# Two more attention pairs on the DMA-transpose path: batch 1, pairs 4 and 5

## The chip, the cores and the metric

One core of a Trainium2 chip runs the whole kernel. The time is device microseconds from launch to end, as the median of several runs. The engines named below are the matmul engine (PE, with its weight loads as PEld), the vector engine (DVE), the scalar engine (ACT), GpSimd (POOL) and the sync engine (SP, which here only issues DMA). Times inside the profile count from the first instruction of the profiled execution.

## The reference

Eight batches of 12 heads, 448 rows, head size 64. Attention with normalized queries and keys, then a low-rank mixing along the sequence, then a two-layer channel network with a residual:

```python
q_n = q / (norm(q) + 1e-6);  k_n = k / (norm(k) + 1e-6)
attn = softmax(q_n @ k_n.T / tau)            # per head, 448 x 448
x = concat_heads(attn @ v)                   # 448 x 768 per batch
u = x + (x.T @ U @ V).T                      # U: 448 x 32, V: 32 x 448
out = u + relu(u @ w_ch1) @ w_ch2            # w_ch1: 768 x 3072, w_ch2: 3072 x 768
```

## The kernel before

The work is cut into 48 **pairs** of heads, numbered `n = 6 * batch + pair` (`NP = 6`), so that batch 1 is n = 6 to 11. One pair takes these steps:

- **Preparation** on a group of two pairs (`Prep`, group 6 is n = 10 and 11, group 7 is n = 12 and 13): squares on POOL, sums on DVE (`reduce`), the root on ACT (`root`), the reciprocal on DVE (`invert`), then four scalings on POOL (`scale`, line 268) that write the normalized `qk`, and a cast of the values on POOL (`values`).
- **T**: the turn of `qk` into `qkT`. For pairs below `2 * NP` this is eight PE transposes (line 297) and a DVE copy (line 302). For pairs from `2 * NP` on, `by_dma` is true and it is one DMA transpose issued by SP (line 312).
- **Sc**: scores, four chunks of keys, each followed by an exponential on ACT. **V**: attention times values in two halves (lines 373 and 380), each divided by its row sums on DVE (`divide_V`, lines 391 and 392) into `X`.
- **Mixing**. The early way is one pair at a time (`step_A`, `step_H`): four matmuls with U (line 413), four that turn X (line 427), one with V (line 438), and a DVE copy to `u` (line 443). The late way (`step_XT`, `step_A2`, `step_H2`) turns X by DMA (line 458), and mixes two pairs as a couple with small matmuls placed side by side (lines 466 and 480), then adds the turned X on DVE (line 485).

Between these steps PE does the channel network of the batch before, cut into **fill** steps of six matmuls: M1 (line 510, w_ch1 with N = 448) and M2 (line 537, w_ch2 with N = 384). M2 of one output half needs that half of w_ch2, loaded by POOL's queue with a cast (`load_w2`, line 173) in two parts of 12 row blocks.

The order on every engine is written by hand. The main loop runs over n from 6; for each n a list `order` holds steps with weights, and `spread` hands out fill between them by these weights. The dictionary `after` holds side work put at (n, place): the preparations, the loads, and the DMA transposes. A queue executes in program order, so a waiting instruction holds those behind it. `FIRST2` decides from which n the couple way and its own `order` lists are used (`late = n > FIRST2`), and `KEEP = 3` fill steps are held back over a batch's end, to cover the last couple's `H2`.

In batch 1 the fill is the channel network of batch 0. So n = 9 is where M2 of batch 0 starts, with the first half of w_ch2; the second half is needed in n = 11.

Of the kernel before, what the change touches and what calls it, by code (L numbers as in the profile page):

```python
# [22 lines left out]
def kernel(  # L23
# [23 lines left out]
    NP = H // 2  # L47
# [123 lines left out]
    def load_w2(half, n0, n1):  # L171
        cols = slice(half * HC, (half + 1) * HC)
        nc.gpsimd.dma_start(
            out=w2_sb[:, n0:n1, cols],
            in_=moe_w_ch2[n0 * 128:n1 * 128, cols].rearrange("(n p) d -> p n d", p=128))
# [100 lines left out]
            nc.gpsimd.tensor_copy(out=self.flat(v65[self.s])[:, :, 0:D], in_=self.flat(vst[self.s]))  # L276


    qkT = {}

    def by_dma(n):

        return n >= 2 * NP

    tp_of, sc_of = {}, {}

# [19 lines left out]
    def step_T(b, p):  # L306
        if not by_dma(b * NP + p):
            pe_T(b, p)
            evict_T(b, p)
            return  # L310
        gi, j = group_of[(b, p)]
        nc.sync.dma_start_transpose(
            out=new_qkT(b, p).rearrange("p a (c r) -> p (a c) r", r=128),
            in_=norm[gi][0][:, j, :, :, :, :].rearrange("p i c h d -> p (i c h d)"))
# [17 lines left out]
    def step_S3(b, p):  # L332

        for i, (nm, tag) in enumerate((("av", "ps_av"), ("up", "ps_x"))):
            t = qkT[(b, p + i)]
            bank = psum.tile([128, 512], FP, name=nm, tag=tag, bufs=1)
            sc_of[(b, p + i, 3)] = bank.unsqueeze(1)
            for h in range(2):
                r, o = slice(64 * h, 64 * h + 64), 64 * (h ^ i)
                nc.tensor.matmul(out=bank[o:o + 64, 0:S], lhsT=t[r, 1, 384 + o:448 + o],  # L340
                                 rhs=t[r, 0, 0:S], start=True, stop=True)
        est.pe(0.19)
        for i in range(2):
            exp_S(b, p + i, 3)

    def exp_S(b, p, c):
        e = E[(b * NP + p) % 2]
        sc = sc_of.pop((b, p, c))
        if c == 3:
            nc.scalar.activation(out=last_of(b, p)[:, 0:S], in_=sc[:, 0, 0:S], func=AF.Exp)  # L350
            est.act(0.56)
        else:
            nc.scalar.activation(out=e[:, 2 * c:2 * c + 2, 0:S], in_=sc[:, :, 0:S], func=AF.Exp)  # L353
            est.act(0.93)

    def step_S(b, p, cs):
        for c in cs:
            pe_S(b, p, c)
            exp_S(b, p, c)
# [217 lines left out]
    pairs = [(b, p) for b in range(B) for p in range(NP)]  # L577
# [9 lines left out]
    def load_all(gi):  # L587
        if gi < len(groups):
            for x in ("q", "k", "v"):
                load(gi, x, nc.sync)  # L590
# [13 lines left out]
    def T(n):  # L604
        step_T(*pairs[n])

    def Sc(n, *cs):
        step_S(*pairs[n], cs)

    def V(n, half):  # L610
        step_V(*pairs[n], half)

    def A(n):
        step_A(*pairs[n])

    def Hs(n):
        step_H(*pairs[n])
# [112 lines left out]
    def put(n, at, fn):  # L730
        after.setdefault((n, at), []).append(fn)

    for gi in range(5, len(groups)):
        m, g = first_pair[gi], preps[gi]
        if m == NP + 2:
            at = [(NP, 1), (NP, 2), (NP + 1, 6), (NP, 5), (NP + 1, 0), (NP + 1, 1)]
            when = (NP + 1, 2)
        elif m == NP + 4:
            at = [(NP + 2, 0), (NP + 2, 1), (NP + 2, 6), (NP + 2, 4), (NP + 2, 6), (NP + 2, 7)]
            when = (NP + 3, 0)  # L740
        elif m == 2 * NP:
            at = [(m - 3, 6), (m - 2, 0), (m - 1, 0)] + [(m - 2, i) for i in (1, 3, 4)]
            when = (m - 2, 5)
        elif m == 2 * NP + 2:
            at = [(m - 2, i) for i in (0, 0, 6, 3, 4, 5)]
            when = (m - 2, 6)
        else:
            at = [(m - 3, 0), (m - 3, 0), (m - 3, 5)] + [(m - 2, i) for i in (0, 1, 2)]
            when = (m - 2, 3)

        put(*at[0], lambda g=g: g.square(0))
        put(*at[1], lambda g=g: g.square(1))
        put(*at[2], lambda g=g: g.values())
        put(*at[3], lambda g=g: g.reduce(0))
        put(*at[4], lambda g=g: g.reduce(1))
        put(*at[5], lambda g=g: g.root())
        put(*when, lambda g=g: (g.invert(), [g.scale(i, j, P_) for j in (0, 1) for i in (1, 0)]))
        if gi > 5 and m - 6 <= NP:
            put(*((NP, 3), (NP + 3, 0))[gi - 6], lambda gi=gi: load_all(gi))
        elif gi > 5:  # L760
            at = {2 * NP + 2: [(m - 4, 5), (m - 4, 6), (m - 3, 2)],
                  2 * NP + 4: [(m - 4, i) for i in (0, 2, 4)]}.get(m, [(m - 6, 4), (m - 5, 5), (m - 4, 3)])
            for x, w in zip("qkv", at):
                put(*w, lambda gi=gi, x=x: load(gi, x, nc.sync))
        if by_dma(m):
            put(m - 1, -1, lambda m=m: T(m))
            put(m - 1, 0, lambda m=m: T(m + 1))

    put(NP, 2, lambda: load_w1(2304, 3072))
    put(NP, 3, lambda: (load_w2(0, 0, 12), load_w2(0, 12, 24)))  # L770
    put(NP + 1, 2, lambda: (load_w2(1, 0, 12), load_w2(1, 12, 24)))
    put(NP + 3, 0, load_copies)
    put(NP + 5, 6, place_copies)

    def spread(n, order, nf, first=0):

# [9 lines left out]
            f(min(want - given, len(fill)))  # L786
            given = want

    FIRST2 = 2 * NP
    KEEP = 3  # L790
    for n in range(NP, NPAIR + 1):
        b, p = pairs[n] if n < NPAIR else (B, 0)
        now, nxt = n < NPAIR, n + 1 < NPAIR
        done = n > NP
        late = n > FIRST2
        for g in after.pop((n, -1), []):
            g()
        state_of["busy"] = n == NP + 1
        if not late:
            if n % 2 == 0:  # L800

                order = [
                    (1, lambda: Sc(n, 0, 1)),
                    (0, done and (lambda: V(n - 1, 0))),
                    (1, None if by_dma(n + 1) else (lambda: T(n + 1))),
                    (0, lambda: Sc(n, 3)),
                    (1, (lambda: V(n - 1, 1)) if done else None),
                    (0, done and (lambda: A(n - 1))),
                    (1, lambda: (Sc(n, 2), Sc(n + 1, 0))),
                    (1, (lambda: Hs(n - 1)) if done else None),  # L810
                ]
            else:
                order = [
                    (1, lambda: Sc(n, 1, 2)),
                    (1, lambda: V(n - 1, 0)),
                    (0, lambda: Sc(n, 3)),
                    (1, lambda: V(n - 1, 1)),
                    (1, not by_dma(n + 1) and (lambda: T(n + 1))),
                    (1, lambda: A(n - 1)),
                    (0, lambda: Hs(n - 1)),  # L820
                ]
            last = p == 0 and done
            nf = len(fill) if last else 5
            spread(n, order, nf)
            if last:
                f(len(fill))
                fill.extend(steps_m1(b - 1) + steps_m2(b - 1))
            continue

        def X2(m):  # L830
            step_XT(*pairs[m])

        def A2(m):
            step_A2(*pairs[m])

        def H2(m):
            step_H2(*pairs[m])

        if n % 2 == 0:
            order = [  # L840
                (2, now and (lambda: (step_S3(*pairs[n]), Sc(n, 0, 1)))),
                (2, lambda: V(n - 1, 0)),
                (2, lambda: (V(n - 1, 1), X2(n - 1))),
                (2, None),
                (3, lambda: (A2(n - 2), now and (Sc(n, 2), Sc(n + 1, 0)))),
                (2, not now and (lambda: H2(n - 2))),
            ]
            nf = len(fill) if not now else int(round((len(fill) - KEEP) / (1 + (-p) % NP)))
            spread(n, order, nf)
            if not now:  # L850
                f(len(fill))
                fill.extend(steps_m1(b - 1) + steps_m2(b - 1))
            continue
        Sc(n, 1, 2)
        if n - 3 >= FIRST2:
            H2(n - 3)
        for g in after.pop((n, 0), []):
            g()
        if p == 1 and n - 2 > FIRST2:
            f(len(fill))  # L860
            fill.extend(steps_m1(b - 1) + steps_m2(b - 1))
        order = [
            (2, lambda: V(n - 1, 0)),
            (2, None if n > FIRST2 + 1 else (lambda: Sc(n, 3))),
            (2, lambda: (V(n - 1, 1), X2(n - 1))),
            (2, None),
            (2, None),
        ]
        nf = int(round((len(fill) - KEEP) / (1 + (-p) % NP)))
        f(2)  # L870
        spread(n, order, nf - 2, 1)
# [37 lines left out]
```

## Time and profile before

| what | value |
|---|---|
| median of 3 runs | 583.81 us (583.78 to 583.82) |
| profiled span | 581.2 us |
| PE busy | 569.7 us, 98% of the span |
| DVE, ACT, POOL busy | 214.3, 260.7, 215.3 us |
| granted PE clock | 0.998 |
| DMA transposes of qk | 36, landing in 3.1 to 6.0 us |
| loads of a quarter of w_ch2 | 4, landing in 23.3 to 31.1 us |

PE is busy nearly always, and matmuls are pipelined, so its busy time says little of lost time. What is lost is read from the chain of waits and from the distance between the starts of neighbouring matmuls.

In the trace the steps of the stretch concerned start at these times on PE: n = 8 at 63.4 us, n = 9 at 72.5, n = 10 at 81.0, n = 11 at 90.8, n = 12 at 98.3, n = 13 at 112.5.

### The profile page before, as it was taken

What the parts mean: (1) busy time and instruction counts of PE and PEld (TensorE: products, weight loads), DVE (VectorE), ACT (ScalarE), POOL (GpSimd) and SP (SyncE); (2) the same over time, 40 slices, a digit from 0 to 9 for tenths busy, and PEclk for the clock granted to TensorE, in tenths of its full rate; (3) what the DMA queues carried; (4) which work ended last, traced back from release to release, by engine and by line L of the source; (5) the groups of instructions that cost most, each with busy time, mean ns of one, the idle gap of its engine ahead of it and who ended that gap; (6) DMA issues with size and microseconds to landing.
All of it is one profiled execution on the core that took longest, in us unless ns stands there. A gap on an engine that the chain in (4) does not pass through costs nothing.

```text
span 581.2 us, 12255 instructions
## 1 busy us (share of the span) xinstructions
PE 569.7 (98%) x5080; PEld 328.7 (57%) x5080; DVE 214.3 (37%) x462; ACT 260.7 (45%) x447; POOL 215.3 (37%) x205
## 2 busy tenths in 40 slices
PE   7999999999999999999999999999999999999997
PEld 6665556655565556555655555655566555655564
DVE  7874552433243334423324343432244332320011
ACT  5877545455433554446424455246443374214200
POOL 8754865706326146326055163253261420000000
PEclk9999999999999999999999999999999999999999
DMA  6899999646376485585375663773754640231012
GB/s 165 195 248 236 239 210 223 178 95 137 98 162 145 93 158 112 135 163 112 80 160 133 132 137 96 144 175 79 136 131 111 132 74 18 52 74 32 11 45 56
DMA packets 138585, 74.25 MB, mean 128 GB/s; under 512 B 85568, under 2 KB 138352, under 8 KB 138528
## 3 DMA queue, kind: packets, MB, share of 16 engines
q1 hardware_dynamic: 128256, 62.77, 48.9%
q0 software_dynamic: 9728, 10.18, 10.3%
q8 instruction: 40, 0.66, 0.5%
q10 hardware_dynamic: 544, 0.51, 0.3%
q14 instruction: 17, 0.14, 0.1%
HBM read 52.19 MB, written 11.01 MB: 109 GB/s over the span
## 4 chain that ended last, share of the span: by engine, by line
PE 89%; DMA 6%; DVE 2%; ACT 1%; SPq 1%; POOL 1%; issue 0%; DVEq 0%; ACTq 0%
PE mp L537 38%; PE mp L510 34%; PE sc L328 5%; DMA w_sb<-in_moe_w_ch_dram 5%; PE av L380 3%; PE up L380 2%; PE av L373 1%; PE av L340 1%; PE sc L650 1%; PE up L373 1%; PE up L466 1%; DMA qst<-in_q_dram 1%; DVE ss L248 1%; PE av L480 1%; PE tp L297 0%; DVE qkT L302 0%
## 5 line engine op out<-in xcount | busy, mean ns | idle before, releaser
L537 PE MATMUL mp<-w_sb,relu 128*128 128x384 bf16 x1344 | 233.7, 326 | 0.2 <-DMA w_sb<-in_moe_w_ch_dram 0.2
L537 PEld LDWEIGHTS <-relu 128*128 128x128 bf16 x1344 | 125.3, 98 | 89.3 <-issue 13.1
L510 PEld LDWEIGHTS <-w_sb 128*128 128x128 bf16 x1128 | 105.0, 98 | 99.5 <-issue 10.0
L514 ACT ACTIVATE relu<-mp 128x448 bf16<-128x448 f32 x161 | 87.6, 544 | 127.8 <-PE mp L510 127.8
L268 POOL TENSOR_TENSOR qk<-kst,inv 128x512 bf16<-128x512 f32 x43 | 46.0, 1070 | 241.9 <-DVE inv L262 241.9
L353 ACT ACTIVATE E<-sc 128x896 bf16<-128x896 f32 x144 | 125.1, 922 | 21.9 <-PE sc L328 20.8
L510 PE MATMUL mp<-uO,w_sb 128*128 128x448 bf16 x576 | 114.3, 353 | 0.0
L510 PE MATMUL mp<-uE,w_sb 128*128 128x448 bf16 x552 | 112.9, 353 | 0.0
L555 DVE TENSOR_TENSOR o_sb<-mp,ut 128x384 f32<-128x384 f32 x50 | 27.9, 558 | 141.3 <-PE mp L537 137.1
L248 DVE TENSOR_REDUCE ss<-sq 128x16 f32<-128x1024 f32 (+1 forms) x50 | 57.9, 1165 | 0.8 <-ACT sq L240 0.7
L268 POOL TENSOR_TENSOR qk<-qst,inv 128x512 bf16<-128x512 f32 x44 | 47.4, 1078 | 1.6 <-PE up L438 1.6
L516 DVE TENSOR_SCALAR relu<-mp 128x448 bf16<-128x448 f32 x27 | 16.9, 625 | 81.2 <-PE mp L510 80.7
L380 PEld LDWEIGHTS <-E 128*128 128x128 bf16 x1152 | 45.0, 97 | 0.0
L328 PE MATMUL sc<-qkT 64*64 64x448 bf16 x576 | 42.4, 359 | 0.6 <-ACT E L353 0.3
L243 POOL TENSOR_TENSOR sq<-kst 128x1024 f32<-128x1024 f32 (+1 forms) x23 | 42.7, 1858 | 0.1
L243 POOL TENSOR_TENSOR sq<-qst 128x1024 f32<-128x1024 f32 x21 | 39.9, 1900 | 3.2 <-DMA qst<-in_q_dram 3.2
L350 ACT ACTIVATE E<-av 128x448 bf16<-128x448 f32 x17 | 9.2, 541 | 47.3 <-PE up L340 47.3
L380 PE MATMUL av<-v,E 128*128 128x65 bf16 x648 | 29.1, 193 | 0.0
L276 POOL CAST v<-vst 128x1024 bf16<-128x1024 f32 (+1 forms) x25 | 25.1, 1006 | 7.7 <-DMA vst<-in_v_dram 6.1
L373 PEld LDWEIGHTS <-E 128*128 128x128 bf16 x192 | 18.1, 98 | 14.7 <-issue 0.8
L470 ACT CAST A_sb<-up 128x128 bf16<-128x128 f32 x18 | 4.8, 264 | 45.9 <-PE up L466 45.9
L391 DVE RECIPROCAL rd<-av 128x4 f32<-128x4 f32 x54 | 9.7, 180 | 42.3 <-PE av L380 42.3
(99 smaller groups left out, 351.2 us busy)
## 6 DMA issues: line engine op xcount, KB each, us to landing
out_dram<-o_sb SPq DMA_DIRECT2D x109, 96.0 KB, 2.2
w_sb<-in_moe_w_ch_dram POOLq DMA_DIRECT2D x8, 1152.0 KB, 18.5
qst<-in_q_dram SPq DMA_DIRECT2D x23, 256.0 KB, 3.8
vst<-in_v_dram SPq DMA_DIRECT2D x46, 128.0 KB, 2.9
kst<-in_k_dram SPq DMA_DIRECT2D x44, 128.0 KB, 2.8
qst<-in_q_dram SPq DMA_DIRECT2D x23, 192.0 KB, 4.0
vst<-in_v_dram SPq DMA_DIRECT2D x46, 96.0 KB, 2.7
kst<-in_k_dram SPq DMA_DIRECT2D x44, 96.0 KB, 2.7
```

The lines of the kernel that those rows point to most:

```text
L243: nc.gpsimd.tensor_mul(sq[:, 0:self.nh * 4, :], self.flat(t), self.flat(t))
L248: nc.vector.reduce_sum(self.ss[:, j, 0:self.nh * 4], self.sq[j][:, 0:self.nh * 4, :], axis=AX.X)
L268: eng.tensor_mul(qks[self.gi % 2][:, j, i, :, :, :], t[:, 2 * j:2 * j + 2, :, :].rearrange("p h c d -> p c h d"), iv.unsqueeze(3).to_broad ...
L276: nc.gpsimd.tensor_copy(out=self.flat(v65[self.s])[:, :, 0:D], in_=self.flat(vst[self.s]))
L328: nc.tensor.matmul(out=sc[o:o + 64, h, 0:S], lhsT=t[r, 1, c * 128 + o:c * 128 + o + 64], rhs=t[r, 0, 0:S], start=True, stop=True)
L353: nc.scalar.activation(out=e[:, 2 * c:2 * c + 2, 0:S], in_=sc[:, :, 0:S], func=AF.Exp)
L373: nc.tensor.matmul(out=av[:, i, :, :], lhsT=last_of(b, p)[:, ic * 128:(ic + 1) * 128], rhs=vv[:, 2 * j:2 * j + 2, 3, :], start=(i == 0), s ...
L380: nc.tensor.matmul(out=av[:, i, h, :], lhsT=e[:, 2 * c + h, ic * 128:(ic + 1) * 128], rhs=vv[:, 2 * j + h, c, :], start=False, stop=(i == ...
L510: nc.tensor.matmul(out=mp, lhsT=w1_sb[:, cc, f * 128:(f + 1) * 128], rhs=u[:, cc, 0:S], start=(cc == 0), stop=(cc == CC - 1))
L514: nc.scalar.activation(out=relu[:, f, o:o + S], in_=mp, func=AF.Relu)
L537: nc.tensor.matmul(out=mp, lhsT=relu[:, f, r0:r0 + 128], rhs=w2_sb[:, f, half * HC:(half + 1) * HC], start=(f == 0), stop=(b > 0 and f == ...
L555: nc.vector.tensor_add(o.rearrange("p (k d) -> p k d", d=128), mp.rearrange("p (k d) -> p k d", d=128), ut_of[(b, half)][:, :, c, :])
```

## The change

Pairs 10 and 11 (the last two of batch 1) go to the late way: their `qk` is turned by two DMA transposes in place of 16 PE transposes and two DVE copies, and they are mixed as a couple, their X turned by DMA. For this the code splits the old bound in two: `FIRST2 = NP + 4` for the turn and the couple, and `FIRST4 = 2 * NP + 2` for the fourth score chunk, which stays as it was for n = 10 to 13.

So that the DMA transposes of 10 and 11 can be issued in n = 9, group 6 is prepared sooner (all of it in n = 8), and group 7 too; the load of the second half of w_ch2 moves from n = 7 to n = 8, behind the squares of group 6, so that POOL has these done first.

```diff
+    FIRST2 = NP + 4
+    FIRST4 = 2 * NP + 2
     def by_dma(n):
-        return n >= 2 * NP
+        return n >= FIRST2
...
         if m == NP + 2:
-            at = [(NP, 1), (NP, 2), (NP + 1, 6), (NP, 5), (NP + 1, 0), (NP + 1, 1)]
+            at = [(NP, 1), (NP, 2), (NP + 2, 1), (NP, 5), (NP + 1, 0), (NP + 1, 1)]
             when = (NP + 1, 2)
         elif m == NP + 4:
-            at = [(NP + 2, 0), (NP + 2, 1), (NP + 2, 6), (NP + 2, 4), (NP + 2, 6), (NP + 2, 7)]
-            when = (NP + 3, 0)
+            at = [(NP + 2, 0), (NP + 2, 0), (NP + 2, 6), (NP + 2, 3), (NP + 2, 4), (NP + 2, 5)]
+            when = (NP + 2, 6)
         elif m == 2 * NP:
-            at = [(m - 3, 6), (m - 2, 0), (m - 1, 0)] + [(m - 2, i) for i in (1, 3, 4)]
+            at = [(m - 3, 6), (m - 3, 6), (m - 1, 0)] + [(m - 2, i) for i in (0, 1, 2)]
+            when = (m - 2, 3)
+        elif m == 2 * NP + 2:
+            at = [(m - 2, i) for i in (0, 0, 5, 2, 3, 4)]
             when = (m - 2, 5)
-        elif m == 2 * NP + 2:
-            at = [(m - 2, i) for i in (0, 0, 6, 3, 4, 5)]
-            when = (m - 2, 6)
...
         if by_dma(m):
-            put(m - 1, -1, lambda m=m: T(m))
-            put(m - 1, 0, lambda m=m: T(m + 1))
+            put(m - 1, 1 if m == FIRST2 else -1, lambda m=m: T(m))
+            put(m - 1, 3 if m == FIRST2 else 0, lambda m=m: T(m + 1))
...
-    put(NP + 1, 2, lambda: (load_w2(1, 0, 12), load_w2(1, 12, 24)))
+    put(NP + 2, 1, lambda: (load_w2(1, 0, 12), load_w2(1, 12, 24)))
...
-    put(NP + 5, 6, place_copies)
+    put(NP + 5, 5, place_copies)
...
-    FIRST2 = 2 * NP
...
-                (2, now and (lambda: (step_S3(*pairs[n]), Sc(n, 0, 1)))),
+                (2, now and (lambda: (n >= FIRST4 and step_S3(*pairs[n]), Sc(n, 0, 1)))),
...
-                (2, None),
+                (2, None if n >= FIRST4 else (lambda: Sc(n, 3))),
...
-            (2, None if n > FIRST2 + 1 else (lambda: Sc(n, 3))),
+            (2, None if n > FIRST4 else (lambda: Sc(n, 3))),
```

The list `at` gives the places of: squares of q, squares of k, values, sums of q, sums of k, root; `when` is the place of the reciprocal and the four scalings. With `late` true from n = 11, batch 0's last fill is now shared out as 6 steps in n = 11, 7 in n = 12 and the 3 kept ones at the start of n = 13, where it was 5 and 11.

More of the change, by code (lines that the diff above doesn't have):

```diff
@@ L817 @@
                     (1, lambda: V(n - 1, 1)),
-                    (1, not by_dma(n + 1) and (lambda: T(n + 1))),
+                    (1, None if by_dma(n + 1) else (lambda: T(n + 1))),
                     (1, lambda: A(n - 1)),
```

## The prediction

> **What bounds the kernel now.** I read the shares of the chain that ended last, then the same chain in order of time around the edited steps, then what PE waited for, then the DMA queues in the same stretch. The chain's shares by engine:
>
> ```profile
> PE 89%; DMA 6%; DVE 2%; ACT 1%; SPq 1%; POOL 1%; issue 0%; DVEq 0%; ACTq 0%
> ```
>
> PE sets the end, but not alone: DMA and DVE hold parts of the chain. The chain in order of time (start, length, what) shows where:
>
> ```profile
> 50.13 29.54 DMA w_sb<-in_moe_w_ch_dram
> 79.71 1.14 PE mp L537 x6
> 80.84 0.19 PE up L438
> 81.03 0.50 PE sc L328 x8
> 81.54 1.08 PE mp L537 x6
> 82.62 0.18 PE mp L547 x3
> 82.82 0.56 DVE o_sb L553
> 83.38 0.13 DVE rd L391
> 83.54 0.42 DVE X L392
> 83.96 1.13 DVE ss L248
> 85.09 0.60 DVE qkT L302
> 85.69 1.13 DVE ss L248
> 86.94 0.44 DVE X L392
> 87.41 0.38 PE av L413 x4
> ```
>
> Two links matter. The second part of w_ch2's first half, issued at 50.13, lands at 79.67, and the third M2 step of batch 0 starts on it at 79.71. So whatever PE saves between 50 and 79.7 us is lost again in this wait. Then DVE carries the path from 82.82 to 87.41: A of pair 9 (line 413) waits for X of pair 9, which stands behind two sums and the qkT copy of pair 11. What PE lost there:
>
> ```profile
> PE av L413 <- DVE X L392: 1.1, 1, 1.1
> PE mp L537 <- DMA w_sb<-in_moe_w_ch_dram: 0.2, 1, 0.2
> ```
>
> By the starts of neighbouring matmuls the two cost 1.22 us (1.378 where 0.162 is usual) and 0.39 us (0.422 where 0.028 is usual). After 113 us I find no start later than its usual distance, up to the end; so the result is the shift of n = 13, and nothing later adds to it.
>
> The DMA queues, first in 62 to 72 us, then in 76 to 80, then in 96 to 98 (packets, MB, share):
>
> ```profile
> q0 software_dynamic: 1532, 1.16, 74.1%
> q1 hardware_dynamic: 1506, 1.23, 48.3%
> ...
> q0 software_dynamic: 1070, 0.81, 130.6%
> q1 hardware_dynamic: 11, 0.01, 0.9%
> ...
> q1 hardware_dynamic: 1614, 0.40, 90.9%
> ```
>
> The reader is to see that the rings are never idle before 94 us, that POOL's queue (q0, the weights) and SP's (q1) go packet for packet while both have work, and that alone a weight packet takes 4 us x 16 / 1070 = 60 ns of one ring. In 96 to 98 us it is the transposes of pairs 12 and 13, which the packet records show as 1024 packets of 256 B each; about 14 ns a packet, 0.9 us a transpose, with the rings to themselves.
>
> **What the Trainium skill says.** "TensorE: Matmul & The Clock Gate", Part 1: warm matmuls start N / 2.4 + about 2.5 ns apart; the trace agrees (56 ns for N = 128, 189 for 448, 162 for 384). "TensorEngine Tiling (Array Packing)", Key Properties: changing the tiling mode drains the engine; the trace agrees (256 ns from an M2 matmul to a 64x64 one, where 162 is usual). "DMA: Bandwidth & Descriptors", Queues, rings and completion order: each DMA engine takes turns between the queues it has work for, packet by packet; the equal counts above agree. The same page, SWDGE vs HWDGE vs iDMA: a packet may hold several descriptors, up to 4096 B; no run here shows how many a transpose has.
>
> **The change part by part.**
>
> *PE work.* Removed: 16 transposes x 56 ns = 0.90 us; two A of 4 x 56 = 0.45; two turns of X of 0.19 = 0.39; two H of 0.189 = 0.38; sum 2.12. Added: one A2 (eight small matmuls, and the mode changes before and after; 0.23 more than the mode changes it replaces) and one H2 of 0.19, together 0.42. I counted the built order of PE with the trace's usual distance for each neighbouring pair: 569.04 us before, 567.34 after, with the wait of 79.7 taken out of its class. So **1.70 us** less, of which T of pair 10 (0.45) comes before the wait at 79.7, T of pair 11 (0.44) lies beside the DVE chain, and 0.81 comes after 87.4.
>
> *T of pair 10 off PE.* PE reaches the third M2 step 0.45 us sooner (78.84) and waits there for the weights. Worth nothing by itself.
>
> *DVE chain to A of pair 9.* In the built order sums of q now go before o_sb, beside other work; then o_sb, X, sums of k, the wait for root on ACT, the two operations of invert, and only then the second X. From the start of o_sb: 0.56 + 0.16 + 0.42 + 1.13, root 0.62 with its hand-overs (86.81 to 87.43 before), invert 0.55, reciprocal and X 0.63, hand-over 0.05: 4.12 us, where it was 87.41 - 82.82 = 4.59. So the wait stays (PE would be there 1.17 us earlier), and **0.47 us** is gained where 0.44 of PE work was removed. E of chunk 3 stands behind root on ACT; it is needed only by V of pair 10, 5 us later.
>
> *Couple mixing after 87.4.* **0.81 us**, straight off PE, if nothing waits. X by DMA: issued near 99 and 105, landing some 2.5 to 4 us later (2.5 is the median), needed at about 110. H2's adds on DVE (2 x 0.62) and the copy of 1.02 lie beside the three kept M2 steps (2.9 us), as in all later batches. The bank `up` for the second half of V is free then.
>
> *Earlier group 6.* Squares at 62.1 to 65.9 on POOL, sums at 67.0 and 68.7 on DVE, root near 69.9, invert until 71.1, scalings 71.15 to 75.2. The first sum goes before X of pair 7, which ends at about 68.71 where it ended at 68.66; A of pair 7 is at 68.96: no wait. The exponentials of n = 8 go 0.6 us later on ACT; their banks are needed at 72.5 and free at 72.15. Nothing.
>
> *Second half of w_ch2 issued at 67 instead of 62.* It stands in POOL's queue behind the first half, which ends at 79.67 either way: it landed at 85.41 and 94.27, is needed at about 96 and 99. Nothing.
>
> *DMA transposes of 10 and 11.* This is the new cost. Issued at 73.3 and 75.3, behind value loads in q1 whose last ring lands at 76.93, and in turn with the end of the very weights that PE waits for. On the slowest ring some 2.6 us of weights are left at 76.5. Low end, one for one at 60 + 16 = 76 ns: 43 packets x 16 = 0.7 us later. High end, transposes in bundles: both get through first, 1.8 us later. The transpose of 10 itself then ends at 76.5 + 64 x 76 ns = 81.4, lands about 0.6 later at 82.0, while Sc of pair 10 wants it at 80.96. No transpose runs beside weights in this trace, so this is bounded, not read. I take 1.1 us for the larger of the two delays (0 to 2.5 for the range). Behind Sc wait V of pair 9, o_sb and so the whole DVE chain. Pair 11 lands near 87, needed at 88 or later: hidden.
>
> *Transposes of 12 and 13.* They landed at 97.53 and 98.42, and Sc of 12 came at 98.28, a margin of 0.75. The two new transposes add 2 x 64 x 14 to 20 ns = 1.8 to 2.6 us to each ring before them: landing 99.3 to 100.1. Sc of 12 now comes at 98.28 + 1.1 - 0.47 - 0.61 + 0.97 (one more fill step ahead of it) = 99.3. Wait 0 to 0.9; I take 0.4.
>
> Sum: -0.47 - 0.81 + 1.1 + 0.4 = +0.2 us: **584.0 us**.
>
> **The rivals.**
>
> *A, the transposes ride for free*: the weights land as before, pair 10 in time, pair 12 in time. Then -0.47 - 0.81 = -1.28: **582.5 us**, 0.22% faster. For it: a transpose needs only 0.9 us of the rings. Against: the rings are full.
>
> *B, a new wait takes the place*: the transposes lose more against the weights, at 100 ns and more a packet, or hold up the rings (in 94 to 96 us pair 12's first half went, and the rest only when the last ring was free). Then delay 2.5 and wait 0.9 and up: +2.1 and more, **586.0 us**, slower. For it: a load that shares the rings takes 104 ns a turn. Against: loads are three to four times larger than these packets.
>
> *C, both old waits vanish*: -1.70 - 0.39 - 1.22 = -3.3, **580.5 us**. It needs the weights sooner, and nothing in their queue before them changes.
>
> **How the numbers follow.** The forecast's case (from -1.1 to +1.1 us) gets 0.46, A 0.20, B 0.30, C 0.04. Range 582.4 to 586.0: it takes in A and most of B, and leaves out C and the worst of B. Faster is A and C, 0.24; slower is B, 0.30.
>
> **What would show it.** Right: M2's wait on the weights over 0.5 us, PE's wait for X near 1.2 still there, a wait of Sc on qkT by DMA at 81 to 83 us, a landing of pair 10's transpose over 5 us, no wait after n = 13. Wrong: weights that land before 79.9 and pair 10 before 80.9 (A), or a wait of over 1.5 us on qkT at n = 10, 11 or 12 (B), or a wait of H2 for the turned X, which I took as hidden.

## The result, and the profile after

| | median us | ratio to before, 95% interval |
|---|---|---|
| before | 583.79 | |
| the change, 4 executions | 586.10 (585.77 to 587.43) | 1.0048 (1.0029 to 1.0066) |
| the change again, 22 executions | 586.17 (585.57 to 588.16) | 1.0036 (1.0023 to 1.0049) |

The change makes the kernel 0.4% slower, about 2.4 us. Both intervals leave out "no difference". The profiled span is 585.6 us (before 581.2). The profiled execution of the change is the slowest of the four (587.43 us, the others 585.77 to 586.19), so its trace shows more than the median loss.

Although 22 matmuls fewer are recorded, PE's busy time rises from 569.7 to 571.6 us. Two rows of the page of after, the span in 40 slices of 14.6 us, show where to look (PE's busy tenths, and the clock that PE was granted):

```profile
PE   7999979999999999999999999999999999999997
PEclk9999989999999999999999999999999999999999
```

The sixth slice, 73 to 88 us, has both a PE that stands still and a clock that is not full. In the page of before the same clock digit is a 9. What PE waited for, in after (total, times, longest, in us):

```profile
PE mp L539 <- DMA w_sb<-in_moe_w_ch_dram: 3.8, 1, 3.8
...
PE av L415 <- DVE X L394: 0.9, 1, 0.9
```

Before, the same two rows had 0.2 and 1.1. The chain of waits of after, in order of time, from the landing of the weights on:

```profile
51.65 31.43 DMA w_sb<-in_moe_w_ch_dram
83.08 0.04 issue
83.12 2.08 PE mp L539 x6
85.20 0.37 PE up L440
85.57 0.89 PE sc L330 x8
86.47 2.04 PE mp L539 x6
88.50 0.32 PE mp L549 x3
...
92.53 0.43 DVE X L394
92.96 0.04 issue
93.00 0.38 PE av L415 x4
```

The second part of w_ch2's first half lands at 83.08, where before it was 79.67. And every PE step after it has about twice its usual length: six M2 matmuls take 2.08 us, not the 1.14 that they took before, and the eight score matmuls 0.89, not 0.50. By the stretches of the trace of after (length, then busy time and instructions of PE, PEld, DVE, ACT, POOL; then PE's clock, the DMA share and GB/s):

```profile
76.50:79.50 3.00, 2.84 (x34) 1.97 (x32) 0.61 (x2) 1.06 (x3) 2.99 (x4) 1.00 1.28 206
82.10:88.90 6.80, 5.78 (x27) 2.55 (x27) 1.79 (x3) 1.73 (x2) 0.00 (x0) 0.50 1.29 193
88.90:93.00 4.10, 3.17 (x41) 2.14 (x39) 3.24 (x8) 0.98 (x3) 0.40 (x1) 0.99 1.30 197
```

For 6.8 us the granted clock is 0.50. Neighbouring M2 matmuls are then 320 ns apart instead of 162. So a busy PE is here a slow PE: the rise in busy time is no added work.

The queues of after in 78 to 84 us (packets, MB, share of 16 engines):

```profile
q0 software_dynamic: 1114, 0.84, 91.0%
q1 hardware_dynamic: 1112, 0.28, 38.4%
```

q0 holds the weights, q1 the two transposes. They get the rings in equal numbers of packets, 1114 to 1112. A pair of packets takes 6 us x 16 / 1113 = 86 ns of a ring, where a weight packet alone took 60. So each 256-byte transpose packet costs the weights about 26 ns, and costs its own transfer 86 ns.

Where the time came in, by the starts of PE's steps in the profiled executions (us; the distances are worked out from them). The third and fifth columns belong to experiments told below: the couple mixing and the sooner preparation with the turn left on PE, and the change with filler work in the wait.

| | before | couple, turn on PE | the change | with filler | the change again |
|---|---|---|---|---|---|
| start of n = 9 | 72.54 | 73.00 | 72.84 | 72.45 | 72.40 |
| to Sc of pair 10 | 8.42 | 8.88 | 12.66 | 12.42 | 11.15 |
| from there to A of pair 9 | 6.45 | 5.88 | 7.50 | 5.88 | 7.76 |
| from there to n = 11 | 3.43 | 3.43 | 3.43 | 3.43 | 3.43 |
| from there to n = 12 | 7.44 | 7.80 | 7.88 | 7.80 | 8.18 |

Two rows carry the loss. Sc of pair 10 comes later, because of the transfers; in the first trace of the change 1.1 us of it is the clock already, since from the M2 step that waited to Sc of pair 10 it took 2.38 us (83.12 to 85.50) where the kernel with the turn on PE took 1.26 (80.62 to 81.88). And from there to A of pair 9 the change takes longer than that kernel, because of the clock. The last row holds one more fill step from the new shares (0.97 us). After n = 13 no start is later than its usual distance, in any of these traces.

### The profile page after: what moved, and what is told of

Its sections match the earlier page's. It is cut to its first block, busy times and chain, and to the rows that moved or that the text cites. A ratio compares the mean times of both kernels' runs of the same rounds, so it can differ in the third digit from the quotient of the medians.

```text
span 585.6 us, 12219 instructions
## 1 busy us (share of the span) xinstructions
PE 571.6 (98%) x5058; PEld 328.4 (56%) x5058; DVE 212.3 (36%) x459; ACT 261.1 (45%) x447; POOL 215.2 (37%) x205
## 3 DMA queue, kind: packets, MB, share of 16 engines
q0 software_dynamic: 9728, 10.18, 10.3%
## 4 chain that ended last, share of the span: by engine, by line
PE 87%; DMA 7%; SPq 2%; DVE 1%; POOL 1%; ACT 1%; issue 1%; POOLq 0%; DVEq 0%
PE mp L539 38%; PE mp L512 33%; DMA w_sb<-in_moe_w_ch_dram 5%; PE sc L330 5%; PE av L382 3%; PE up L382 2%; DMA kst<-in_k_dram 1%; PE av L375 1%; PE av L342 1%; PE up L375 1%; PE up L468 1%; PE av L482 1%; DMA vst<-in_v_dram 1%; SPq L213 0%; DVE X L394 0%
## 5 line engine op out<-in xcount | busy, mean ns | idle before, releaser
L375 PEld LDWEIGHTS <-E 128*128 128x128 bf16 x192 | 18.1, 98 | 14.6 <-issue 1.0
```

Source lines behind the costliest of these rows:

```text
L375: nc.tensor.matmul(out=av[:, i, :, :], lhsT=last_of(b, p)[:, ic * 128:(ic + 1) * 128], rhs=vv[:, 2 * j:2 * j + 2, 3, :], start=(i == 0), s ...
```

## The experiments

My theory after the result: the loss is the DMA turn alone, first by the ring time that it takes from the weights, then by the clock that drops in the wait; the couple mixing and the sooner preparation gain what I had worked out. The rivals: the couple mixing or the new places of the preparation cost something; or the loss is in what waits for `qkT`, not in the ring time.

**One part undone: the turn back on PE.** Couple mixing and preparation stay.

```diff
     def by_dma(n):
-        return n >= FIRST2
+        return n >= 2 * NP
...
-        if half == 1 and by_dma(b * NP + p):
+        if half == 1 and b * NP + p >= FIRST2:
```

> The change, but pairs 10 and 11 are turned by PE as before; the couple mixing, the X turned by DMA and the earlier preparation stay. Contention theory (the two new DMA transposes take turns with the first half of w_ch2 on the rings and so lengthen PE's wait for it): the weights' second part lands as in the kernel before (near 79.7, within 1 us), and the time is 0.3 to 1.3 us below before, 582.5 to 583.5. Rival, couple mixing (H2 or A2 waits, KEEP too small): slower than before by 1.5 us or more, like the change. Rival, preparation order: slower as well.

Measured: 582.17 us, ratio 0.9972 (0.996 to 0.9983): faster than before by 1.5 us, a little more than expected. PE's waits in this kernel:

```profile
PE mp L539 <- DMA w_sb<-in_moe_w_ch_dram: 0.7, 1, 0.7
...
PE av L415 <- DVE X L394: 0.5, 1, 0.5
```

The wait on the weights is 0.7 us instead of 3.8, and that on X of pair 9 is half of what it was before the change. So the turn by DMA costs (1.0036 - 0.9972) x 583.7 = 3.7 us, by the measurement of the change with more executions, and the rest of the change is a gain.

**The other part undone: single mixing, turn by DMA.**

```diff
-    FIRST2 = NP + 4
+    FIRST2 = 2 * NP
...
     def by_dma(n):
-        return n >= FIRST2
+        return n >= NP + 4
...
```

The lines left out keep the places of the two transposes and of the bank for V as these bounds ask.

> The change, but pairs 10 and 11 are mixed one at a time as before; their turn by DMA and the earlier preparation stay. Contention theory: PE waits over 2 us for the weights at the third M2 step, pair 10's transpose takes over 9 us to land, and the time is 2 to 4 us above before, 585.8 to 587.8. Rival, couple mixing: no slower than before.

Measured: 587.58 us, 1.0068 (1.0055 to 1.0081). In its trace PE waited 2.8 us for the weights and 2.1 for `qkT` in two waits, and the clock was halved for 3.4 us. Without the couple mixing the change is slower still, by (1.0068 - 1.0036) x 583.7 = 1.9 us. That is more than the 0.8 of PE work that the mixing saves; part of it is a wait of 1.6 us for the turn of pair 12, which ended at 103.66 us; in the two traces of the change that wait is 0.1 and 0.4. The rest was not followed up.

**The cost alone: the kernel before, with two more transposes that nobody reads.** They turn `qk` of pairs 8 and 9 once more (the second in two halves), into tiles that are not read, and have as many packets as those of the change. The function `idle_T`, which issues them, is left out here.

```diff
+    put(NP + 3, 1, lambda: idle_T(0))
+    put(NP + 3, 3, lambda: idle_T(1))
```

> The kernel before, with extra DMA transposes of the qk of pairs 8 and 9 into buffers that nobody reads, issued by SP after the loads of n = 9, as many packets as the change adds; nothing waits for them. Contention theory: the second part of the weights' first half lands 1.5 to 2.5 us later than in before, and since that landing is on the path the time is 1.5 to 3 us above before, 585.3 to 586.8. Rival (the loss comes from the order of preparation or of mixing): as before, within 0.4 us.

Measured: 587.42 us, 1.0069 (1.0055 to 1.0082), 3.8 us above the kernel before on the same chip (583.66), more than expected. What PE waited for in it:

```profile
PE mp L537 <- DMA w_sb<-in_moe_w_ch_dram: 3.9, 1, 3.9
...
PE av L413 <- DVE X L392: 1.1, 1, 1.1
```

This is what settles it. No instruction waits for these transposes, and yet they cost all of the 3.7 us. So the loss needs no wait on `qkT`; the wait on the weights grew from 0.2 to 3.9 us, and the clock was halved for 3.4 us after it. The wait for X of pair 9 stands as before. It does not need the clock either: two of the five executions had a mean clock of 1.0, and took 587.31 and 587.42 us.

Not all of the longer wait in this trace is the sharing of turns. The first unread transpose was issued at 71.86, 1.7 us sooner than that of pair 10 in the change. And between 77 and 78 us the rings all but stood still:

```profile
q0 software_dynamic: 45, 0.03, 95.7%
q1 hardware_dynamic: 55, 0.02, 93.8%
```

That is 100 packets in 1 us, where from 79 to 83 us it was some 380 in each. What stopped them is not shown.

**The preparation alone: the kernel before, with the new places.**

```diff
...
-            when = (NP + 3, 0)
+            when = (NP + 2, 6)
...
-    put(NP + 1, 2, lambda: (load_w2(1, 0, 12), load_w2(1, 12, 24)))
+    put(NP + 2, 1, lambda: (load_w2(1, 0, 12), load_w2(1, 12, 24)))
```

> The kernel before with the new places of preparation and of the load of w_ch2's second half alone; turn and mixing as before. Contention theory: no slower, -0.6 to +0.3 us. Rival, preparation order (POOL or DVE late, weights issued late): slower by 1.5 us or more.

Measured: 583.03 us, 0.999 (0.9981 to 0.9998). PE's waits:

```profile
PE av L413 <- DVE X L392: 0.5, 1, 0.5
PE mp L537 <- DMA w_sb<-in_moe_w_ch_dram: 0.5, 1, 0.5
```

A gain of 0.6 us (583.66 - 583.03), which the interval holds from 0.1 to 1.1, by a shorter wait for X of pair 9. The couple mixing then adds 583.03 - 582.17 = 0.9.

**The clock alone: filler matmuls in the wait.** 55 matmuls of the identity, into a bank of the scores that is written anew before it is read, stand before the third M2 step.

```diff
+    def warm(k):
+        t = psum.tile([128, 2, 512], FP, name="sc", tag="ps_sc", bufs=2)
+        for _ in range(k):
+            nc.tensor.matmul(out=t[:, 0, 0:128], lhsT=ident, rhs=ident, start=True, stop=True)
+
+    put(NP + 3, 5, lambda: warm(55))
```

> The change, with 55 matmuls of the identity into an unread bank put on PE where it waits for the weights (some 3.1 us of work in a wait of 3.8). Theory that PE's clock is halved after the long wait, and that this adds to the loss: no window of half clock near 82 us, and the time falls by 1 to 2 us against the change, to 584.1 to 585.1. Rival (the wait alone is the loss): as the change, 586.1, or slower by what the matmuls overrun.

Measured: 585.31 us, 1.0023 (1.0014 to 1.0033), just above the expected range. The mean granted clock was 0.998 or more in all 22 executions; in the change alone it was in 4 of 22. The stretch that had 0.50 above, in this trace:

```profile
82.10:88.90 6.80, 5.11 (x61) 3.14 (x60) 3.89 (x6) 1.73 (x2) 0.00 (x0) 1.00 1.34 173
```

And what PE waited for:

```profile
PE sc L330 <- DMA qkT<-qk: 1.7, 1, 1.7
...
PE av L415 <- DVE X L394: 0.9, 1, 0.9
```

So with work added to PE the change is faster, by 0.8 us. The two were timed on different chips, and the intervals of their ratios to before overlap, so the clock is the surer finding here, and the 0.8 us an estimate. It does not make the change faster than before: the transfers still hold it up, now by the turn of pair 10 itself, which landed at 84.83. Within the 22 executions of the change, the four with a mean clock of 0.998 or more have a median of 585.76 and the others 586.24. So the clock is worth about 0.5 to 0.8 us of the median. In the two profiled executions of the change it took more, 2.7 and 1.9 us (the third row of the table against 5.88, and in the first trace the 1.1 us before it). Why the executions without it are not faster by as much is open: of those, no trace was taken.

**Other traffic out of the way: the values of group 7 behind the transposes.**

```diff
...
+                put(NP + 3, 0, lambda: (load(7, "q", nc.sync), load(7, "k", nc.sync)))
+                put(NP + 3, 4, lambda: load(7, "v", nc.sync))
```

> The change, with the value loads of group 7 behind the two new transposes in SP's queue. Contention theory: these four loads shared the rings with the weights one for one, at some 44 ns a packet and 28 packets a ring, so without them the weights' second part lands about 1.2 us sooner, PE's wait falls below 3 us, no window of half clock follows, and the time is 1 to 3 us below the change, 583.1 to 585.1. Rival (the transposes slow the rings by themselves, whatever else is queued): as the change, within 0.5 us.

Measured: 585.83 us, 1.0035 (1.0025 to 1.0044): a miss. PE's waits in it:

```profile
PE sc L330 <- DMA qkT<-qk: 3.5, 2, 2.5
...
PE mp L539 <- DMA w_sb<-in_moe_w_ch_dram: 2.1, 1, 2.1
```

The weights landed at 81.43 and pair 10 at 83.70, both sooner than in the change as profiled (83.08 and 84.77). But PE then stood waiting for Sc of pair 12 from 101.1 on, 2.5 us long: the transpose of pair 12 landed at 103.58, between the 104.26 and the 102.88 of the two traces of the change. What was gained at pair 10 was lost there. That the value loads, now nearer to that transpose, are what kept it late was not tested.

This trace shows one thing more. The queues from 74.8 to 77.5 us:

```profile
q0 software_dynamic: 719, 0.55, 131.5%
q1 hardware_dynamic: 4, 0.00, 0.4%
```

The transpose of pair 10 was issued at 73.67, and the loads ahead of it in SP's queue were through by 75.1; yet its first packet ran at 77.60, 3.9 us after the issue, while the weights had the rings alone.

**The same on the kernel with the turn on PE**, with the values behind the first output.

```diff
...
+                put(NP + 4, 1, lambda: load(7, "v", nc.sync))
```

> Couple mixing with the turn by PE, and the value loads of group 7 behind the first output of batch 0. Contention theory: the weights land about 1.2 us sooner than in the couple run, PE no longer waits for them, and the time is 0.2 to 0.8 us below that run, 581.4 to 582.0. Rival (the weights' landing is not on the path there any more): as the couple run, 582.2; or slower if the later loads make pair 12 late.

Measured: 581.36 us (580.95 to 582.05), 0.9957 (0.9941 to 0.9974), at the edge of what was expected. The weights land at 78.14 instead of 80.58, and PE has no wait on them left. The 0.8 us between the two versions is not clear of noise: they were timed on different chips, and the intervals of their ratios overlap. This version beats both kernels, by 2.2 us and by (1.0036 - 0.9957) x 583.7 = 4.6 us.

**The second half of w_ch2 later**, in n = 9 instead of n = 8, so that it would not stand against the turn of pair 11.

```diff
-    put(NP + 2, 1, lambda: (load_w2(1, 0, 12), load_w2(1, 12, 24)))
+    put(NP + 3, 6, lambda: (load_w2(1, 0, 12), load_w2(1, 12, 24)))
```

> The change, with the second half of w_ch2 issued behind the squares of group 7 (near 81 us instead of 67), so that once the first half is through the rings nothing takes turns with the two transposes. Contention theory: pair 11's transpose lands before 87 us instead of at 90 or later, pair 10's before 84 instead of near 84.7, the first half's second part as in the change, and the time is 0.5 to 2 us below the change, 584.1 to 585.6 (less the gain if pair 12's transpose or the second half becomes late). Rival (DMA transposes are slow whatever is beside them): pair 11 still lands 14 us or more after its issue, time as the change.

Measured: 586.97 us, 1.0046 (1.0035 to 1.0058): a miss in time, 0.8 us above the change on the same chip. The landing moved as expected, pair 11 at 85.46 instead of 91.51. But nothing waited for pair 11, the first half still landed at 83.65 and PE waited 3.5 us for it. Why it is slower than the change was not found.

**The change once more**, unchanged, in 22 executions on the same chip as the last one.

> The change as it is, timed beside the run with the late second half, and with a second trace: 585.5 to 586.6. If the half clock after the wait is part of the loss, the runs spread by over 1 us, and the trace shows such a window only where PE's wait for the weights is above some 3.4 us; if it is no part, no window or no difference.

Measured: 586.17 us, 1.0036, as expected. The executions spread over 2.6 us, and the clock was halved for 6.8 us, though no single wait was as long as the 3.4 us that I had thought it takes. This profiled execution is near the median, and it splits the loss in another way:

```profile
PE mp L539 <- DMA w_sb<-in_moe_w_ch_dram: 2.3, 1, 2.3
PE sc L330 <- DMA qkT<-qk: 1.4, 2, 1.1
```

The weights came at 81.11 and pair 10 at 83.51. These waits come to 3.7 us, 0.3 of it for pair 12, where the first trace had one wait of 3.8. Which of the transfers PE meets differs between these two executions. The landings of all traces (us), with the distance between the two parts of the first half, since the whole timetable of transfers shifts by up to 2 us between executions:

| | part 1 | part 2 | distance | turn of pair 10 |
|---|---|---|---|---|
| before | 72.53 | 79.67 | 7.14 | (on PE) |
| preparation alone | 72.80 | 80.09 | 7.29 | (on PE) |
| couple, turn on PE | 74.17 | 80.58 | 6.41 | (on PE) |
| the same, late values | 72.61 | 78.14 | 5.53 | (on PE) |
| unread transposes | 74.05 | 84.23 | 10.18 | (on PE) |
| the change | 73.77 | 83.08 | 9.31 | 73.60 to 84.77 |
| the change again | 72.82 | 81.11 | 8.29 | 73.16 to 83.51 |
| single mixing | 73.33 | 82.06 | 8.73 | 73.60 to 83.92 |
| with filler | 73.06 | 80.82 | 7.76 | 73.21 to 84.83 |
| late values | 74.06 | 81.43 | 7.37 | 73.67 to 83.70 |
| late second half | 74.48 | 83.65 | 9.17 | 74.41 to 84.55 |

With transposes beside them the weights take 7.4 to 10.2 us, without 5.5 to 7.3 (with the value loads in their old place, 7.8 to 10.2 and 6.4 to 7.3). And the turn of pair 10 takes 10.0 to 11.6 us, where before the turns of `qk` took 3.1 to 6.0. In every trace part 1 landed before the first transpose packet ran (at 76.03 with the unread transposes, at 77.2 or later in the others), so where it is late the transposes are not the reason: of the 3.4 us by which part 2 came later in the first trace than in before, 1.2 are of this kind.

## Why the prediction was wrong

The forecast was 584.0 us, and 586.1 came out, just past the top of the range and on rival B's number: a new wait takes the place, by transposes that lose against the weights and hold up the rings. I gave B 0.30. That its number came out so well is in part luck. Its delay of 2.5 us is what the traces show; its 100 ns a turn and its wait of 0.9 us for pair 12 are not (86 ns, 0.1 to 0.4 us), and the clock, which was in no sum, made up for them.

- *PE work, 1.70 us less, of which 0.81 counts after 87.4*: right. From the preparation alone to the couple with the turn on PE the gain was 0.9.
- *T of pair 10 off PE, worth nothing by itself*: right. In the change PE stands waiting for the weights in that place, longer than before.
- *DVE chain to A of pair 9, -0.47*: right. The preparation alone gained 0.6, and PE's wait for X fell from 1.1 to 0.5. The wait that I expected to stay near 1.2 in the change read 0.9, and it is not in the rows of the second trace.
- *Earlier group 6 and the second half of w_ch2 later, nothing*: right. The kernel with both alone is not slower.
- *Transposes of 12 and 13, wait 0.4*: right in size. By the last row of the table Sc of pair 12 waited 0.1 and 0.4 us in the two traces of the change. X by DMA was hidden, as said.
- *DMA transposes of 10 and 11, "I take 1.1 us"*: this step failed; the term was less than half of what came. Against the kernel with the turn on PE, Sc of pair 10 came 3.8 us later after the start of n = 9 in the first trace and 2.3 in the second (12.66 and 11.15 against 8.88). Without the 1.1 us of clock in the first, the transfers cost 2.7 and 2.3 us. Two terms of the landing were too small. I had the packets of pair 10 start at 76.5, 3.2 us after the issue, as soon as the value loads were through. In all six traces in which pair 10 is turned by DMA they started 3.9 to 4.3 us after it, with late values too, so the value loads are not the whole reason; the turns of X, which come when the rings are less full, mostly start 1.2 us after theirs. And I had 76 ns a turn, as 60 + 16; it was 86. With the 0.6 us that I had from the last packet to the landing, 4.1 + 64 x 0.086 + 0.6 = 10.2 us from issue to landing, where 8.7 was predicted and 10.0 to 11.6 were read. Pair 11 landed at 91.51 and 90.28, not near 87, but nothing waited for it.
- *A term that I had not in the sum at all*: the clock. A longer wait is not only its own length: in both traces of the change PE had half clock for 6.8 us, and in 18 of 22 executions the mean clock was under 0.998. By the filler matmuls that is some 0.8 us of the median. I had quoted the row on the granted clock of before, 0.998, and did not ask what would hold it there once PE waits.

The sum redone with these numbers: -0.6 (chain) - 0.9 (mixing) + 2.3 to 3.5 (weights and turn of 10; the 3.5 is from the trace with filler, 12.42 against 8.88) + 0.1 to 0.4 (pair 12) + 0.5 to 0.8 (clock) = +1.4 to +3.2, with 2.4 measured. What I call the clock's share is bounded by two measurements that don't agree closer than that, and the split between the two transfers differs between executions; neither was narrowed further.

In the reasoning, the error was to let a transpose packet cost the weights about what it takes alone (16 ns, where 26 was measured), and to let the transposes start as soon as the loads ahead of them were through. The profile of before had said what decides: between 62 and 94 us no ring was idle. For a full ring the question is how much ring time the new packets take in all, and who stands last in line.

The Trainium skill, "DMA: Bandwidth & Descriptors", Queues, rings and completion order, holds that each engine turns between its queues packet by packet. The trace bears this out to 2 packets in 1100. It follows that a transfer of small packets gets half of the turns, whatever its bytes. Whether anybody reads what it brings makes no difference to that, which is why the unread transposes cost as much as the read ones.

## What to carry to other kernels

Before work is moved from a busy engine to DMA, look at the DMA queues of just those microseconds: where the rings are full, count packets, not bytes, and price each at its turn with the neighbour, to both of them. Then ask who waits for the transfer that shares the rings, since an unread transfer can cost as much as a read one. And where a wait of PE grows by 2 us or more, look at the granted clock in it and after it; here it was cheaper to give PE something to do there than to leave it idle, and better still not to have the wait.

## What the runs showed of the hardware

- A DMA transpose of 1024 packets of 256 B, which takes about 0.9 us of the rings alone, took 10 to 16 us from issue to landing beside a weight load with a cast: the turn with one weight packet is 86 ns a ring, against 14 for a transpose packet alone and 60 for a weight packet alone. Its first packet ran 3.9 to 4.3 us after the issue, with the rings full of weights, even where its own queue had moved nothing for 2.5 us; a turn of X with no weights beside it started after 1.2 us. What that time goes into was not tried.
- The clock can fall with waits shorter than I would have thought. The Trainium skill, "TensorE: Matmul & The Clock Gate", Part 1, puts the half rate after at least one idle window of about 3.4 us. In the trace with the unread transposes the clock fell 3.8 us into the wait, which fits. In the first trace of the change it fell 2.8 us into the wait (82.13, with PE idle from 79.34), and with the late second half 2.0 us into it. In the second trace of the change two waits of 2.3 and 1.1 us with a step of M2 between them were enough. What the five falls in these traces share is the 3.4 us before each: PE was busy for 0.0 to 1.4 us of them. With the filler the emptiest 3.4 us still had 1.7 us of work, in the kernel before 2.4, and there was no fall. But the kernel with late values had as little as 0.9 us in one such stretch, and full clock in its profiled execution (in 18 of its 22 executions the mean clock was under 0.998). So a stretch with little work is not enough by itself; what else decides, such as where the window stands, was not tried. The lengths of the slow stretches, 3.4 and 6.8 us, are one and two of the page's windows.
